# The first nine steps of a retention and mixture-of-depths kernel: one chunk of 128 tokens a step in place of two of 64

## The chip, the cores and the metric

The kernel runs on one core of a Trainium2 chip. Its time is the device time of one execution in microseconds (us). The kernel before was timed three times: 277.89, 277.18 and 274.35 us, median 277.18. One further execution was profiled: 274.87 us, of which 273.2 us are the span that the profile covers. Shorter is better.

## The reference

Eight batches, eight heads, 576 tokens, 64 numbers a head; everything is float32. First a retention layer with decay gamma by head, then a mixture-of-depths layer on the 512 numbers of a token:

```python
scores = scale * np.matmul(q, k.transpose(0, 1, 3, 2))
Dmat = np.where(rel >= 0, gamma[:, None, None] ** rel[None, :, :], 0.0)
x = np.matmul(scores * Dmat[None], v)          # then heads side by side: (8, 576, 512)
s = np.einsum('bsd,d->bs', x, w_gate)
out = x.copy()
for b in range(B):
    top_idx = np.argpartition(-s[b], 128)[:128]
    xe = x[b, top_idx]
    ye = np.maximum(xe @ w1, 0.0) @ w2         # 512 -> 1024 -> 512
    g = 1.0 / (1.0 + np.exp(-s[b, top_idx]))
    out[b, top_idx] = xe + g[:, None] * ye
```

So every token gets its retention value, and the 128 tokens of each batch with the highest gate scores get an MLP on top.

## The kernel before

**Retention by chunks.** A chunk is 64 tokens of one batch, all heads; a batch has 9 chunks. A step `s` takes two chunks, so 36 steps do all 72, and a batch ends after 4.5 steps. The host packs q and k (transposed), v and k for a step into one 1 MB block, `raw[s]`: [128, 4, 512], heads 0 to 3 on one half of the partitions and heads 4 to 7 on the other. In a step:

- `scaled` (L151, on POOL; in steps 5 to 7 on ACT in eight pieces, L147): v times a power of gamma, `vs`.
- `scores` (L175): 16 matmuls of 64x64, k against q, into PSUM `sc_ps`.
- `masked` (L232, DVE): causal mask, PSUM to SBUF `am`.
- `update` (L165): 16 matmuls add k times v to the running state `u_ps`; `copied` (L205, ACT) brings the state to SBUF, `st`, after each chunk.
- `crosswise` (L186, L196): 32 matmuls into `y_ps`: the masked scores times `vs`, and q times the state before the chunk. They are recorded one step late, between the scores and updates of the next step (`block`), so that PE need not wait for the mask.
- `values` (L241, L250, DVE): `y_ps` times a power of gamma to `xs`, and the gate score of each token as sums over two half rows.
- `store` (L259, POOL queue): `xs` to the output, two transfers a step.

**Choice of tokens for a batch.** `total` (L281) adds the half sums, `spread` (L296, L301) puts the 576 scores in a row on every partition, five `compare` (L309, DVE) count for each token how many score higher, `one_hot` (L322, DVE) and `rows` (L330) turn the ranks into 128 row numbers, and `gather` (L339, an indirect transfer on the POOL queue) reads these rows of the output back. It must wait until the batch's stores have landed. For batch 0 two special steps, `first` (s = 4) and `second` (s = 5), do part of this early.

**MLP for a batch.** `turn` (L356) transposes the gathered rows, four `up` parts (L365, 16 matmuls of 128x128 each) and four `down` parts (L373, 4 matmuls with 512 columns each) follow, and a scatter writes the rows. The parts are dealt out over the steps of the following batches, one or two at the end of a step (`share`); batch 0's start in step 8, batch 1's in step 13, batch 2's in step 18.

**Order.** Each engine runs its instructions in the order in which the Python code issues them; nothing is rescheduled. Loads go through the SP queue, stores and gathers through the POOL queue. `raw` has 8 buffers: step s+7's load waits for step s-1. `bring` issues loads in pieces of 256 KB; for steps 0 to 5 (`few`) it lets a piece wait for an earlier one, so that at most five are under way:

```python
while len(flying) > 3 + few:
    flying.popleft()
if few and len(flying) == 4:
    tc.add_manual_dep(ins, flying.popleft().name, ...)
```

Of the kernel before, what the change touches and what calls it, by code (L numbers as in the profile page):

```python
# [16 lines left out]
P = 128  # L17
TINY = 2.0**-125
C = 64
# [4 lines left out]
def layout(H, NC, cap):  # L24

    at, n = {}, 0
    for name, size in (("dec", 2 * (NC + 1) * H // 2), ("causal", C), ("wgh", H * C // 2),
                       ("pair", C), ("place", (NC + 1) // 2)):
        at[name] = n
        n += size  # L30
    at["end"] = n
    return at
# [3 lines left out]
def kernel(  # L36
# [16 lines left out]

    nc = tc.nc
# [13 lines left out]
    assert cap == P and cap < S <= 1024 and NC % 2 == 1  # L68
# [20 lines left out]
    flying = deque()  # L89

    def bring(out, in_, few=False):

        ins = nc.sync.dma_start(out=out, in_=in_).ins
        while len(flying) > 3 + few:
            flying.popleft()
        if few and len(flying) == 4:
            tc.add_manual_dep(
                ins, flying.popleft().name,
                mybir.DependencyInfo(mybir.DependencyClass.Sync, mybir.DependencyReason.DATA),
                reason="few transfers at a time")  # L100
        flying.append(ins)

    def load(s):
        x = loads.tile([P, 4, DM], F32, name="raw")
        for a in range(4):
            bring(x[:, a, :], qkvk[s, :, a * DM : (a + 1) * DM], few=s <= ends[0])
        raw[s] = x
# [5 lines left out]
    place = const.tile([P, NK], F16, name="place")  # L113

    dec = table[:, : col["causal"]].rearrange("p (s h) -> p s h", s=2)
# [4 lines left out]
    ahead = const.tile([P, 2 * S - C], F32, name="ahead")  # L120
    slots = const.tile([P, cap], F32, name="slots")
    eye = const.tile([P, P], F32, name="eye")
    ones = const.tile([P, P], F32, name="ones")

    def constants():

        nc.gpsimd.memset(ahead, -TINY)
        nc.gpsimd.affine_select(out=ahead, in_=ahead, pattern=[[-1, 2 * S - C]],
                                compare_op=OP.is_gt, fill=0.0, base=S - C, channel_multiplier=1)
        nc.gpsimd.memset(ones, 1.0)  # L130
        nc.gpsimd.affine_select(out=eye, in_=ones, pattern=[[-1, P]],
                                compare_op=OP.is_equal, fill=0.0, base=0, channel_multiplier=1)
        nc.gpsimd.iota(slots, pattern=[[1, cap]], base=0, channel_multiplier=0,
                       allow_small_or_imprecise_dtypes=True)
# [5 lines left out]
    by_act = lambda s: ends[0] <= s < ends[0] + 3  # L140

    def scaled(s):
        c = batch(2 * s)[1]
        vs[s] = work.tile([P, DM], F32, name="vs")
        if by_act(s):
            for i in range(H):
                nc.scalar.activation(  # L147
                    out=vs[s][:, D * i : D * i + D], in_=raw[s][:, 2, D * i : D * i + D],
                    func=AF.Copy, scale=dec[:, 0, HH * c + i : HH * c + i + 1])
            return  # L150
        nc.gpsimd.tensor_tensor(  # L151
            out=blocks(vs[s]), in0=blocks(raw[s][:, 2, :]),
            in1=dec[:, 0, HH * c : HH * c + H].unsqueeze(2).to_broadcast([P, H, D]), op=OP.mult,
        )
# [115 lines left out]
    full = S // P  # L270
    size = lambda k: P if k < full else S - P * full
# [16 lines left out]
    def spread(b, *groups):  # L288

        if b not in row:  # L290
            row[b] = work.tile([P, S], F32, name="row", bufs=2)
        for group in groups:
            t = bank("row_ps")
            at = 0
            for k, p0, p1 in group:
                nc.tensor.matmul(  # L296
                    t[:, at : at + p1 - p0], rs[b][p0:p1, k : k + 1].to_broadcast([p1 - p0, P]),
                    eye[p0:p1, p0:p1], start=True, stop=True, skip_group_check=True)
                at += p1 - p0
            j = P * group[0][0] + group[0][1]  # L300
            nc.scalar.copy(out=row[b][:, j : j + at], in_=t[:, :at])  # L301

    def compare(b, k, j0=0, j1=S, part=0):
        if b not in rank:
            rank[b] = work.tile([P, 2, NK], F32, name="rank", bufs=2)
        n = size(k)
        scr = work.tile([P, S], F32, name="scr2", bufs=1)
        at = S - C - P * k
        nc.vector.scalar_tensor_tensor(  # L309
            scr[:n, : j1 - j0], row[b][:n, j0:j1], rs[b][:n, k : k + 1],  # L310
            ahead[:n, at + j0 : at + j1],
            op0=OP.subtract, op1=OP.is_gt, accum_out=rank[b][:n, part, k : k + 1])
# [5 lines left out]
    def one_hot(b):  # L318
        hot[b] = work.tile([P, NK, cap], F16, name="hot", bufs=2)
        for n, ks in ((P, slice(0, full)), (size(full), slice(full, NK))):  # L320
            m = ks.stop - ks.start
            nc.vector.tensor_tensor(  # L322
                out=hot[b][:n, ks, :], in0=slots[:n].unsqueeze(1).to_broadcast([n, m, cap]),
                in1=rank[b][:n, 0, ks].unsqueeze(2).to_broadcast([n, m, cap]), op=OP.is_equal)

    def rows(b):
        t = bank("idx_ps")
        for k in range(NK):
            n = size(k)
            nc.tensor.matmul(t[:, :1], hot[b][:n, k, :], place[:n, k : k + 1],  # L330
                             start=k == 0, stop=k == NK - 1)
        idx[b] = work.tile([P, 1], I32, name="idx", bufs=B)
        nc.scalar.copy(out=idx[b], in_=t[:, :1])
# [71 lines left out]
    columns = lambda k0, k1: [(k, 0, size(k)) for k in range(k0, k1)]  # L405
# [3 lines left out]
    def go(fs):  # L409
        for f in fs:  # L410
            f()

    def first():

        s = ends[0] - 1
        block(s)
        masked(s)
        go(crosswise(s, (0,)))
        values(s - 1)
        store(s - 1)  # L420
        total(0, 0, NC - 1)
        spread(0, columns(0, full))
        values(s, (0,))
        total(0, NC - 1, NC)
        spread(0, columns(full, NK))
        go(crosswise(s, (1,)))
        for k in range(full):
            compare(0, k, 0, P * full)

    def second():  # L430
        s = ends[0]
        block(s, False)
        masked(s)
        for k in range(full):
            compare(0, k, P * full, S, 1)
        compare(0, full)
        joined(0, full)
        one_hot(0)
        values(s - 1, (1,))
        store(s - 1)  # L440

    s = ends[0] + 1
    plan(mid, s, rows, 0)
    plan(mid, s, gather, 0)
    plan(early, s + 1, turn, 0)
    plan(late, s + 1, mlp, 0)
    plan(late, s + 1, gates, 0)
    start = [s + 2]
    for b in range(1, last):
        s = ends[b]  # L450
        plan(late, s, total, b)
        plan(early, s + 1, spread, b, columns(0, full), columns(full, NK))
        for k in range(3):
            plan(late, s + 1, compare, b, k)
        for k in range(3, NK):
            plan(mid, s + 2, compare, b, k)
        plan(mid, s + 2, one_hot, b)
        plan(late, s + 2, rows, b)
        plan(late, s + 2, gather, b)
        plan(early, s + 4, turn, b)  # L460
        plan(early, s + 4, mlp, b)
        plan(late, s + 4, gates, b)
        start.append(s + 4)
    plan(late, NS - 1, total, last, 0, NC - 2)
    plan(before, NS, spread, last, columns(0, odd) + [(odd, 0, C)])
# [15 lines left out]
    bring(table, consts)  # L481
    constants()
    for s in range(AHEAD):
        load(s)
    for d in range(KD):
        bring(w1_sb[:, d, :], w1[P * d : P * d + P])
    bring(wg, bass.AP(tensor=w_gate.tensor, offset=w_gate.offset, ap=[[0, P], [1, DM]]))
    scaled(0)
    for s in range(NS + 1):
        if s and s + AHEAD - 1 < NS:  # L490
            load(s + AHEAD - 1)
        if s == 2:
            for d in range(0, FB, 2):
                bring(w2_sb[:, d : d + 2, :],
                      w2[P * d : P * d + 2 * P].rearrange("(a p) d -> p a d", p=P))
        run(before, s)
        if s + 1 < NS and not by_act(s + 1):
            scaled(s + 1)
        if s == ends[0] - 1:
            first()  # L500
        elif s == ends[0]:
            second()
        else:
            block(s)
            if s < NS:
                masked(s)
            run(mid, s)
            if s:
                values(s - 1)
                store(s - 1)  # L510
        if s == 2:
            nc.vector.tensor_copy(out=place, in_=place_f)
        if by_act(s + 1):
            scaled(s + 1)
# [6 lines left out]
    spread(last, [(odd, C, P)], [(full, 0, C)])  # L521
# [3 lines left out]
    compare(last, full)  # L525
# [70 lines left out]
```

## Time and profile before

| | us |
|---|---|
| three timed runs | 277.89, 277.18, 274.35 |
| profiled execution | 274.87 |
| its span | 273.2 |
| busy in the span: PE / DVE / POOL / ACT | 231.0 / 141.7 / 103.3 / 58.7 |
| first scores (L175) | 5.88 |
| masks of steps 0 to 4 | 7.9, 11.7, 15.7, 21.2, 27.4 |
| masks of steps 5 to 9 | 37.8, 42.3, 47.2, 59.3, 64.8 |
| raw loads of 256 KB, median from issue to landing | 5.2 |
| bytes moved | 56.8 MB |

A group line of the profile has the line in the code, the engine, the operation, what it writes and reads, the shapes, the count; then the busy time in us and the mean ns of one; then the idle time of the engine ahead of it and what ended most of it. In the chain of waits each line has a start in us, a length, and what ran or was waited for; "issue" is time in which an engine waited for nothing that the profile shows. The granted clock is the share of full speed that TensorE was given.

### The profile page before, as it was taken

How to read it: one execution, taken by the hardware profiler on the slowest of the kernel's cores; microseconds unless marked ns; L12 is line 12 of the kernel's file. 1: busy time of each engine (PE TensorE's matmuls, PEld its weight loads, DVE VectorE, ACT ScalarE, POOL GpSimd, SP SyncE). 2: the span in 40 equal slices, each digit the busy share in tenths (PEclk: the TensorE clock that was granted, in tenths of full speed). 3: DMA queues.
4: the chain of work that ended last, by engine and by line, in shares of the span. 5: the costliest groups of instructions: out<-in, count | busy, mean ns of one | idle time of the engine just before them, and what ended most of it. 6: DMA issues, size and time to landing. Idle time of an engine off the chain costs nothing.

```text
span 273.2 us, 11548 instructions
## 1 busy us (share of the span) xinstructions
PE 231.0 (85%) x5184; PEld 183.9 (67%) x5184; DVE 141.7 (52%) x354; ACT 58.7 (22%) x182; POOL 103.3 (38%) x138
## 2 busy tenths in 40 slices
PE   1845886089977999969999999699999998999992
PEld 1734785079753897649866986469868975894950
DVE  0333585243593538865864378818736487750101
ACT  1111164032210232113211231112212321121100
POOL 4264202804407353364163741824165525201101
PEclk9998568569998999999999999979999999999998
DMA  6879999999996786586577766866042113211000
GB/s 209 276 244 304 315 409 377 376 406 385 326 390 198 245 280 213 190 277 247 170 229 250 256 218 207 266 221 216 26 114 80 42 43 78 70 49 38 38 2 38
DMA packets 27601, 56.83 MB, mean 208 GB/s; under 512 B 4000, under 2 KB 4128, under 8 KB 27552
## 3 DMA queue, kind: packets, MB, share of 16 engines
q1 hardware_dynamic: 22688, 42.46, 46.6%
q0 software_dynamic: 4864, 13.64, 15.2%
q8 instruction: 41, 0.67, 1.0%
q14 instruction: 8, 0.07, 0.1%
HBM read 44.54 MB, written 11.53 MB: 205 GB/s over the span
## 4 chain that ended last, share of the span: by engine, by line
PE 60%; issue 14%; DMA 13%; DVE 8%; ACT 1%; POOLq 1%; POOL 1%; SPq 0%; DVEq 0%; ACTq 0%
PE h_ps L365 17%; PE ye_ps L373 11%; PE u_ps L165 9%; PE sc_ps L175 9%; DMA xr<-out,idx 7%; DVE scr L309 5%; DMA raw<-in_qkvk 5%; PE row_ps L296 5%; PE y_ps L196 4%; PE y_ps L186 3%; PE xg_ps L356 2%; DVE hot L322 1%; DVE am L232 1%; DMA out<-xs 1%; PE idx_ps L330 1%
## 5 line engine op out<-in xcount | busy, mean ns | idle before, releaser
L259 POOL DMA_DIRECT2D out<-xs x64 | 39.8, 625 | 90.3 <-DVE xs L241 89.9
L232 DVE TENSOR_TENSOR am<-sc_ps,table 128x512 f32<-128x512 f32 x36 | 24.9, 690 | 74.2 <-PE sc_ps L175 53.6
L365 PEld LDWEIGHTS h_ps<-xg,w_sb 128*128 128x128 f32 x512 | 59.5, 192 | 5.5 <-issue 4.4
L373 PE MATMUL ye_ps<-w_sb,hT 128*128 128x512 f32 x128 | 63.0, 624 | 0.0
L365 PE MATMUL h_ps<-xg,w_sb 128*128 128x128 f32 x512 | 62.2, 278 | 0.5 <-issue 0.4
L175 PE MATMUL sc_ps<-raw 64*64 64x64 f32 x1152 | 44.9, 231 | 11.0 <-DMA raw<-in_qkvk 5.9
L175 PEld LDWEIGHTS sc_ps<-raw 64*64 64x64 f32 x1152 | 41.0, 146 | 13.1 <-issue 7.0
L165 PE MATMUL u_ps<-vs,raw 64*64 64x64 f32 x1024 | 45.7, 232 | 3.3 <-ACT st L205 2.4
L186 PE MATMUL y_ps<-vs,am 64*64 64x64 f32 x1152 | 45.9, 232 | 3.0 <-issue 2.7
L309 DVE SCALAR_TENSOR_TENSOR scr<-row,rs,ahead 128x576 f32<-128x576 f32 (+5 forms) x47 | 42.7, 909 | 10.2 <-ACT row L301 6.1
L165 PEld LDWEIGHTS u_ps<-vs,raw 64*64 64x64 f32 x1024 | 38.1, 144 | 11.7 <-issue 6.4
L186 PEld LDWEIGHTS y_ps<-vs,am 64*64 64x64 f32 x1152 | 40.1, 144 | 3.6 <-issue 3.0
L205 ACT COPY st<-u_ps 128x256 f32<-128x256 f32 x64 | 23.7, 371 | 82.3 <-PE u_ps L165 60.9
L196 PE MATMUL y_ps<-st,raw 64*64 64x64 f32 x1024 | 39.7, 227 | 2.0 <-issue 2.0
L151 POOL TENSOR_TENSOR vs<-raw,table 128x512 f32<-128x512 f32 x33 | 34.7, 1052 | 13.3 <-DMA raw<-in_qkvk 12.8
L196 PEld LDWEIGHTS y_ps<-st,raw 64*64 64x64 f32 x1024 | 36.0, 143 | 2.1 <-issue 2.1
L373 PEld LDWEIGHTS ye_ps<-w_sb,hT 128*128 128x128 f32 x128 | 22.8, 195 | 19.5 <-issue 18.7
L250 DVE SCALAR_TENSOR_TENSOR scr<-xs,table 128x256 f32<-128x256 f32 x72 | 34.0, 473 | 2.5
L241 DVE TENSOR_TENSOR xs<-y_ps,table 128x512 f32<-128x512 f32 (+1 forms) x37 | 24.7, 667 | 3.9 <-PE y_ps L196 3.6
L367 ACT ACTIVATE hT<-h_ps 128x256 f32<-128x256 f32 x32 | 12.3, 383 | 55.7 <-PE h_ps L365 55.7
L378 DVE SCALAR_TENSOR_TENSOR o<-ye_ps,gate,xr 128x512 f32<-128x512 f32 x8 | 6.0, 751 | 30.3 <-PE ye_ps L373 17.5
L379 POOL DMA_INDIRECT out<-o,idx x8 | 9.5, 1187 | 31.1 <-DVE o L378 31.1
(35 smaller groups left out, 113.0 us busy)
## 6 DMA issues: line engine op xcount, KB each, us to landing
raw<-in_qkvk SPq DMA_DIRECT2D x144, 256.0 KB, 5.2
out<-xs POOLq DMA_DIRECT2D x64, 128.0 KB, 4.9
w_sb<-in_w SPq DMA_DIRECT2D x8, 512.0 KB, 8.9
out<-xs POOLq DMA_DIRECT2D x16, 64.0 KB, 4.9
wg<-in_w_gate SPq DMA_DIRECT2D x1, 256.0 KB
table<-in_consts SPq DMA_DIRECT2D x1, 234.5 KB
xr<-out,idx POOLq DMA_INDIRECT x8, 4.0
out<-o,idx POOLq DMA_INDIRECT x8, 4.1
```

The lines of the kernel that those rows point to most:

```text
L151: nc.gpsimd.tensor_tensor(out=blocks(vs[s]), in0=blocks(raw[s][:, 2, :]), in1=dec[:, 0, HH * c : HH * c + H].unsqueeze(2).to_broadcast([P, ...
L165: yield lambda h=h, half=half: nc.tensor.matmul(u_ps[b][half, where(0, h)], raw[s][half, 3, where(e, h)], vs[s][half, where(e, h)], start= ...
L175: yield lambda e=e, h=h, half=half: nc.tensor.matmul(sc_ps[s][half, where(e, h)], raw[s][half, 1, where(e, h)], raw[s][half, 0, where(e, h ...
L186: yield lambda e=e, h=h, i=i, half=half: nc.tensor.matmul(y_ps[s][halves[1 - i], where(e, h)], am[s][half, where(e, h)], vs[s][half, where ...
L196: yield lambda g=g, e=e, h=h, i=i, half=half: nc.tensor.matmul(y_ps[s][halves[1 - i], where(e, h)], raw[s][half, 0, where(e, h)], st[g - 1 ...
L232: nc.vector.tensor_tensor(out=blocks(am[s]), in0=blocks(sc_ps[s]), in1=causal.unsqueeze(1).to_broadcast([P, H, C]), op=OP.mult)
L241: nc.vector.tensor_tensor(out=blocks(xs[s])[:, i0:i1, :], in0=blocks(y_ps[s])[:, i0:i1, :], in1=dec[:, 1, HH * c + i0 : HH * c + i1].unsqu ...
L250: nc.vector.scalar_tensor_tensor(scr, xs[s][:, W * e : W * e + W], 1.0, wgh, op0=OP.mult, op1=OP.mult, accum_out=sc[b][:, c : c + 1])
L259: nc.gpsimd.dma_start(out=outs[b][C * c : C * c + 2 * C, W * i : W * i + W] .rearrange("(c p) d -> p c d", c=2), in_=x)
L309: nc.vector.scalar_tensor_tensor(scr[:n, : j1 - j0], row[b][:n, j0:j1], rs[b][:n, k : k + 1], ahead[:n, at + j0 : at + j1], op0=OP.subtrac ...
L365: nc.tensor.matmul(t[:, a, :], w1_sb[:, d, P * (f + a) : P * (f + a) + P], xg[b][:, d, :], start=d == 0, stop=d == KD - 1)
L373: nc.tensor.matmul(ye[b], hT[b][:, a, :], w2_sb[:, a, :], start=a == 0, stop=a == FB - 1)
```

## The change

The first nine steps, which are the first two batches (2 x 576 = 9 x 128 tokens), get their own code. A step takes 128 tokens in their order as one chunk, with tokens on partitions. Step 4 (`middle`) holds the last 64 tokens of batch 0 and the first 64 of batch 1, kept apart by its own mask. There are 32 matmuls a step and one state copy. The scaling of v runs on POOL in all steps. Row sums come out of `values` directly, without `total`. Everything of a step, its `within` matmuls too, is issued in that step, so `block(9)` has no crosswise of step 8. Batch 0's whole ranking is in step 5, its rows and gather in step 6, its transposes at the end of step 7 and its MLP from step 8 on, as before; batch 1's follow one step earlier than before (MLP from step 12). Loads are 512 KB each, with no limit; w1 and w2 come in loads of 1 MB, issued behind the loads of steps 8 and 9 (before: w1 ahead of step 8's load, w2 behind step 9's). The table is 144 columns longer and comes in two parts. A sigmoid on one column runs first on ACT.

```diff
-    def bring(out, in_, few=False):
...
     def load(s):
         x = loads.tile([P, 4, DM], F32, name="raw")
-        for a in range(4):
-            bring(x[:, a, :], qkvk[s, :, a * DM : (a + 1) * DM], few=s <= ends[0])
+        for a in (0, 2):
+            nc.sync.dma_start(out=x[:, a : a + 2, :], in_=qkvk[s, :, a * DM : (a + 2) * DM])
...
+    middle = NC // 2
+    heads = [(hh, j) for j in range(HH) for hh in range(2)]
+    def big_scores(s):
+        am[s] = work.tile([P, H, P], F32, name="am2", bufs=2)
+        sc_ps[s] = [bank("sc_ps", "sc", 2) for _ in range(2)]
+        for hh, j in heads:
+            half = halves[1 - hh]
+            nc.tensor.matmul(
+                sc_ps[s][hh][:, P * j : P * j + P], raw[s][half, 1, P * j : P * j + P],
+                raw[s][half, 0, P * j : P * j + P], start=True, stop=True, skip_group_check=True)
+    def big_masked(s):
+        for hh in range(2):
+            nc.vector.tensor_tensor(
+                out=am[s][:, HH * hh : HH * hh + HH, :],
+                in0=sc_ps[s][hh].rearrange("p (h d) -> p h d", d=P),
+                in1=seen[:, int(s == middle), :].unsqueeze(1).to_broadcast([P, HH, P]),
+                op=OP.mult)
+    def big_update(s):
...
+        for hh, j in heads:
+            h = HH * hh + j
+            nc.tensor.matmul(
+                u_ps[b][halves[1 - hh], where(0, j)], raw[s][rows_, 3, D * h : D * h + D],
+                vs[s][rows_, D * h : D * h + D], start=new and j == 0,
+                stop=s in (middle - 1, NC - 2), skip_group_check=True)
+        st[2 * s + 1] = work.tile([P, W], F32, name="st")
+        nc.scalar.copy(out=st[2 * s + 1], in_=u_ps[b][:, :W])
+    def big_before(s):
...
+        for hh, j in heads:
+            half = halves[1 - hh]
+            nc.tensor.matmul(
+                y_ps[s][hh][:n, where(0, j)], raw[s][half, 0, P * j : P * j + n],
+                st[2 * s - 1][half, where(0, j)], start=s != middle and j == 0,
+                stop=s == middle, skip_group_check=True)
+    def big_within(s):
+        for hh in range(2):
+            for j in range(HH):
+                h = HH * hh + j
+                nc.tensor.matmul(
+                    y_ps[s][hh][:, where(0, j)], am[s][:, h, :], vs[s][:, D * h : D * h + D],
+                    start=s in (0, middle) and j == 0, stop=s != middle, skip_group_check=True)
+    def big_values(s):
+        xs[s] = work.tile([P, DM], F32, name="xs", bufs=4)
+        for hh in range(2):
+            i = HH * hh
+            nc.vector.tensor_tensor(
+                out=blocks(xs[s])[:, i : i + HH, :], in0=blocks(y_ps[s][hh])[:, :HH, :],
+                in1=big[:, 1, s, i : i + HH].unsqueeze(2).to_broadcast([P, HH, D]), op=OP.mult)
+        scr = work.tile([P, DM], F32, name="scr3", bufs=1)
+        nc.vector.scalar_tensor_tensor(scr, xs[s], 1.0, wg, op0=OP.mult, op1=OP.mult,
+                                       accum_out=rs01[:, s : s + 1])
...
-    def first():
...
-    def second():
...
+    def big_step(s):
+        big_ahead(s)
+        if s == middle + 1:
+            spread(0, columns(0, 0, NK - 1), columns(0, NK - 1, NK))
+        if s == middle + 2:
+            rows(0)
+            gather(0)
+        big_masked(s)
+        big_rest(s)
+        if s == middle + 1:
+            for k in range(NK):
+                compare(0, k)
+            one_hot(0)
+        big_values(s)
+        big_store(s)
...
+    warm = work.tile([P, 1], F32, name="warm", bufs=1)
+    nc.scalar.activation(out=warm, in_=ones[:, :1], func=AF.Sigmoid)
     for s in range(AHEAD):
         load(s)
+        if s == 0:
+            nc.sync.dma_start(out=wg, in_=bass.AP(...))
+        if s == 2:
+            nc.sync.dma_start(out=table[:, n_big:], in_=consts[:, n_big:])
...
+        if s < NC:
+            big_step(s)
         else:
-            block(s)
+            block(s, s > NC)
```

`big_ahead(s)` issues the scores, `big_before` (q times the state) and `big_update`, in this order; `big_rest(s)` issues `big_within`. In step 4, `big_before` comes after `big_within`. `big_store` writes 128 rows in one transfer (two in step 4). The two banks of `sc_ps` and the two of `y_ps` are all that these steps have, so step s+1's scores wait for step s's masks, and its `before` for step s's values.

## The prediction

> **What bounds the kernel now.** I read first the page's strip of 40 slices (6.83 us each), to see where TensorE is not full.
>
> ```profile
> PE   1845886089977999969999999699999998999992
> PEclk9998568569998999999999999979999999999998
> GB/s 209 276 244 304 315 409 377 376 406 385 326 390 198 245 280 213 190 277 247 170 229 250 256 218 207 266 221 216 26 114 80 42 43 78 70 49 38 38 2 38
> ```
>
> From the tenth slice on PE is nearly always full. Before it PE has holes, and the granted clock falls to 0.5 and 0.6. The transfers move 209 to 315 GB/s in the first five slices and about 380 after that: the start runs below what the queues can carry. The table of stretches says the same.
>
> ```profile
> 20.00:30.00 10.00, 6.24 (x212) 5.91 (x212) 4.38 (x12) 0.74 (x2) 3.84 (x7) 0.74 0.93 306
> 30.00:40.00 10.00, 8.60 (x163) 7.82 (x164) 6.01 (x23) 4.69 (x20) 1.09 (x2) 0.58 1.01 371
> 63.70:118.90 55.20, 51.21 (x1367) 40.08 (x1366) 35.52 (x82) 11.81 (x36) 24.18 (x32) 0.97 0.81 269
> ```
>
> (length, busy PE, PE weight load, DVE, ACT, POOL, clock, transfer share, GB/s). Steps 9 to 17 fill 63.7 to 118.9 us, and there PE is busy for 51.2 of 55.2 us at clock 0.97. The change rewrites the steps before that. The chain of waits, in order of time, says what they wait for.
>
> ```profile
> 2.19 4.26 DMA raw<-in_qkvk
> 6.46 3.46 DMA raw<-in_qkvk
> 9.94 5.18 DMA raw<-in_qkvk
> ...
> 18.64 1.79 issue
> ...
> 23.27 2.89 issue
> ...
> 44.18 1.99 issue
> ...
> 48.73 6.85 DMA xr<-out,idx
> ```
>
> Loads first, then "issue" holes, then batch 0's gather, for which PE stands still 7.5 us (48.15 to 55.63). The issue holes have a count behind them: numbering PE's instructions in order of time, they stand before the 451st, 707th, 963rd and 1,730th, multiples of 256 apart (within one), and the instruction queue moved 41 packets of 16 KB, one for each 256. So PE ran out of fetched instructions: a stretch of small matmuls uses 256 faster than they come.
>
> The line from which both kernels run nearly the same code is the start of step 9, at 63.7 us, behind two parts of batch 0's MLP:
>
> ```profile
> 59.94 3.77 PE h_ps L365 x32
> 63.70 0.20 PE sc_ps L175 x2
> ```
>
> **The change, part by part.** I work out when step 9 starts in the changed kernel.
>
> *First data.* The third transfer in the trace (0.76 MB with those ahead of it) landed at 5.74 us and later ones 0.64 to 0.70 us per 256 KB: bytes flow from about 3.8 us on at 0.38 to 0.4 MB/us. Now a 74 KB table piece and 512 KB of q and k come first: 0.6 MB, 5.3 us; v and k follow at 6.7 us. Transfers of one queue land in order (the four w_sb loads, issued at 31.1 to 33.0 us, land 1.1 to 1.3 us apart behind the raw loads ahead of them), so "no limit" doesn't delay the first.
>
> *Step 0.* Scores 5.4 to 6.7, masks to 7.9, v scaled on POOL (1.05) by 7.8, within to 9.7 (PE at half clock, as in the first step of before), values to 11.0, masks of step 1 to 12.4 us.
>
> *The loop of steps 1 to 8.* PE now waits in each step for its own masks; before, the crosswise matmuls came one step late. DVE in one step:
>
> ```profile
> L232 DVE TENSOR_TENSOR am<-sc_ps,table 128x512 f32<-128x512 f32 x36 | 24.9, 690 | 74.2 <-PE sc_ps L175 53.6 <-PE y_ps L196 17.4 <-PE y_ps L186 3.2
> L347 DVE SCALAR_TENSOR_TENSOR scr<-xr,wg 128x512 f32<-128x512 f32 x8 | 5.5, 682 | 5.8 <-DMA xr<-out,idx 5.8
> L241 DVE TENSOR_TENSOR xs<-y_ps,table 128x256 f32<-128x256 f32 x2 | 0.8, 417 | 0.2 <-PE y_ps L196 0.2
> ```
>
> Two masks at 0.69, two values at 0.417, one score sum at 0.68 + 0.08: 2.97 us, plus 0.1 for the semaphore after the second mask: 3.1 us a step if PE hides. Before it was 0.69 + 0.68 + 2 x 0.55 = 2.5. PE has 32 matmuls. The trace has no 64-row tile with 128 columns in pairs; bounds: a pair runs together (112 ns, as one 128-column h_ps matmul) or one after the other (224). Two 64x64 start 7 ns apart and a pair takes 57 ns, so I take pairs together: scores 0.45 (or 0.9), before and update 0.24 each (or 0.47), within 8 x 0.06 = 0.47; 1.4 us (or 2.3). The old 64 took 64 x 28 ns = 1.8 us. PE thus gains little by itself; at half clock it needs 2.8 (or 4.6) and shows in the loop. PE sits idle about half of each step, and the trace fell to half clock at 24.7 and 45.2 us after stretches of 3.4 us that were 45 and 56% busy, and came back only after stretches of 86 to 100%. A loop that idles at full clock and fills at half will swing: I take 3.5 us, between 3.1 and 5.0.
>
> The Trainium skill (TensorE: Matmul & The Clock Gate, section "HAM oscillation — how this bites in real kernels") warns that idle gaps over about 3.4 us drop the clock; by that rule alone no gap here is long enough and the loop would stay at 3.1.
>
> *Tile modes.* 64x128, 128x64 and 128x128 now alternate three times a step. From a 128x128 h_ps to a 64x64 update the next matmul starts 205 ns later, not 112: 0.09 us a switch, 0.27 a step, inside the wait for the masks; bare it is 2.4 us over nine steps.
>
> *Step 5* carries batch 0's ranking whole: 4 compares at 0.83, one of 64 rows at 0.83, one-hot 0.9: 5.0 us on DVE, with PE waiting for values(5). *Gather:* idx stands 2.3 us after step 5's one-hot (31.4: values, before, update, rows, copy), about 33.7 us; the gather takes 6.85 us as before, 40.6; PE gets there at 38.9, so it stalls 1.7 us in place of 7.5. The stores it waits for are issued by 25 us, not at 43.
>
> *Sum:* 12.4 + 6 x 3.5 + 5.0 + 0.5 = 38.9, stall to 40.6, transposes 0.6, scores, masks and within of step 8 2.8: 44.0; two MLP parts 3.77: 47.8; something for half clock there and in steps 0 to 4: **step 9 starts at 49** (63.7 before). Issue holes: 64 instructions a step make 256 last 13 us; none. The sigmoid load (1.28 us at 57.4, which held a state copy from 57.84 to 58.79) goes: 0.9 us, already inside the 49. The Trainium skill (ScalarE: Activation LUTs, "What ACT_TABLE_LOAD costs") counts a drain of 1.38 us with each load, 2.66 in all; by it the gain would be 1.7 us more, but here the copy began 0.13 us after the load ended. The eight small scalings on ACT in each of steps 5 to 7 go to POOL (1.05 us each), which has one store a step at 0.6 beside them: hidden.
>
> *Transfers set the ceiling.* Until raw 10 the queue carries 0.07 + 11 x 1.05 + 0.5 (wg, rest of the table) + 4.2 (w1, w2) = 16.3 MB, and about 2.5 MB of stores and gather go beside it: 18.8 MB at 0.38 MB/us from 3.8 us on is 53.3 us. Step 10 starts by PE at 49 + 6.0 - 0.9 = 54.1 (69.7 before). So loads follow by a hair, and more than 16.4 us can't be won. From step 11 on a step needs 1.3 MB, 3.5 us, and PE takes 5 to 6.
>
> *From step 9 on* work and order are the same, but for crosswise(8), already done (32 x 28 ns = 0.9 us), batch 1's row sums, and its MLP a step earlier; by step 18 both have done the same parts. So 63.7 - 49 + 0.9 = **15.6 us** stay.
>
> The profiled execution took 274.87 us (span 273.2); 274.87 - 15.6 = 259.3. It lies 2.3 below the median of 277.18; I add half: **260.5**.
>
> **The rivals.**
> - *Half clock, pairs one after the other:* PE needs 4.6 us, the loop 5.0. Step 9 at 49 + 7 x 1.5 = 59.5; gain 5.1; 270. For it: clock 0.58 at 30 to 40 us with PE 86% busy. Against: the 7 ns starts. 0.18.
> - *Loads at 300 GB/s*, as in slices 4 and 5: raw 10 at 3.8 + 18.8 / 0.3 = 66.5, gain 3.2, about 272. Against: 376 to 409 as soon as the limit was gone. 0.10. The edit not doing what it says (transfers sharing instead of in order: first scores at 12.7 with 3.4 MB in flight) costs under 7.4 us and lies between.
> - *Slower: the loop becomes one serial chain at half clock.* Scores 1.8, before and update 1.9, masks 1.4, within 0.95, values 1.6, semaphores 0.4: about 8 us a step with nothing beside it; step 9 at 49 + 7 x 4.5 = 80.5, plus 3.8 for cold MLP parts; 295. It decides from 49 + 7 x (c - 3.5) = 64.6, c = 5.7 us a step, and is slower by 2% from c = 6.5. For it: PE waits for DVE in each step. Against: score banks are free after the masks, so scores run under values. 0.07.
>
> **The numbers.** The forecast has 0.65. About 2% can be told from no change: 271.6 and 282.7 us. Low end: loop 3.1 and loads at the ceiling, 274.87 - 17.3, and PE's wait of 1.38 us at 79 us for batch 1's one-hot saved: 256, less 2 for spread: 254. High end: the first rival, 270. Faster 0.65 + 0.16 + 0.03 = 0.84; same 0.09; slower 0.07.
>
> **What would show it.** First scores near 5.4 us; masks 3.1 to 4 us apart in steps 1 to 4; 9 us between the masks of steps 5 and 6; no issue hole before 49 us; a PE stall under 3 us ahead of batch 0's transposes; 380 GB/s from the second slice on; step 9 near 49 and step 18 near 103 us (118.9). It is wrong if masks lie over 5.7 us apart, or if PE from step 9 on waits for raw.

## The result and the profile after

| | before | after |
|---|---|---|
| median of the runs, us | 276.06 (274.35 to 277.89) | 299.50 (297.29 to 300.50) |
| profiled execution / its span, us | 274.87 / 273.2 | 299.89 / 298.2 |
| start of step 9's scores, us | 63.7 | 83.3 |
| start of step 18's mask, us | 118.4 | 138.4 |
| start of step 27's mask, us | 174.7 | 198.4 |
| PE busy in the span, us | 231.0 | 269.8 |

The kernel became slower: ratio 1.084, interval 1.073 to 1.094. Medians in this text are of all executions, while a ratio to the kernel before, which ran beside each experiment, leaves out executions over 1.5% above the fastest of their kernel. Of the 25 us between the two profiled executions, 19.7 us stand at step 9 already, and 0.3 us are added up to step 18. Another 3.7 us come between steps 18 and 27, where the code is the same in both kernels, and 1.3 us later.

First the page's strip of 40 slices of the kernel after (7.46 us each).

```profile
PE   1999999699999998796999998969999999999993
PEclk9999999955899999899799999997999999999997
GB/s 201 394 403 418 410 397 406 164 206 182 164 52 143 192 301 262 147 213 291 199 181 191 235 267 182 185 269 210 206 40 75 77 70 2 111 70 27 45 0 35
```

The holes in PE are gone, and the transfers run at about 400 GB/s from the second slice on, as forecast. From the eighth slice on they fall to 164 GB/s: loads are no longer asked for, because the steps come too slowly. PE is full, and the time is lost in PE itself. The table of stretches (length, busy PE, PE weight load, DVE, ACT, POOL, clock, transfer share, GB/s) says how few matmuls fill it.

```profile
20.00:30.00 10.00, 10.00 (x73) 9.53 (x74) 3.29 (x8) 0.37 (x1) 1.66 (x2) 1.00 1.03 417
60.00:70.00 10.00, 10.00 (x87) 9.50 (x87) 3.91 (x8) 0.43 (x2) 3.79 (x5) 0.50 0.55 186
83.25:138.90 55.65, 51.65 (x1299) 39.88 (x1298) 33.31 (x79) 11.77 (x35) 21.93 (x29) 0.97 0.61 188
```

PE is TensorE, DVE VectorE, ACT ScalarE and POOL GpSimd. 73 matmul records, which are the matmul entries of the trace, keep PE busy for 10 us. Steps 9 to 17 (the last line) take 55.7 us, against 55.2 before, so the second half of the work is not what changed. The chain of waits, in order of time (start, length, what ran), shows what one costs.

```profile
21.46 2.01 PE sc_ps L157 x16
23.47 1.60 PE y_ps L193 x16
25.07 1.05 PE u_ps L179 x16
26.12 3.61 PE y_ps L202 x16
...
62.27 3.61 PE y_ps L202 x16
...
77.73 1.97 PE y_ps L202 x16
79.70 3.63 PE h_ps L457 x32
83.33 0.72 PE sc_ps L259 x19
```

Lines 157, 193, 179 and 202 are scores, `before`, update and `within`. Step 2, the first four lines, is these four pieces end to end, 8.27 us, with no wait for DVE between them. The same 16 records of `within` take 3.61 us at 26 us and at 62 us, and 1.97 us at 77.7 us. At 62 us the table above gives the clock as 0.50, and at 77.7 us it is full. So the clock was at half at 26 us too, although the strip has a 9 there and the table a 1.00: the first change of clock that the trace holds is at 52.7 us, and ahead of the first change the strip and the table show full speed whatever the clock is. By the distances between matmul records (213 ns in `within` at 26 us) the clock was at half from the start to 52.7 us, and again from 59.5 to 76.6 us.

DVE, which the forecast took for the bound of the loop, has these groups (count, then busy us, mean ns, and the idle time ahead of them).

```profile
L163 DVE TENSOR_TENSOR am<-sc_ps,seen 128x512 f32<-128x512 f32 x18 | 11.6, 684 | 13.6 <-PE sc_ps L157 13.6
L223 DVE TENSOR_TENSOR xs<-y_ps,table 128x256 f32<-128x256 f32 x18 | 7.4, 422 | 31.3 <-PE y_ps L202 27.1 <-PE y_ps L193 4.2
L227 DVE SCALAR_TENSOR_TENSOR scr<-xs,wg 128x512 f32<-128x512 f32 x9 | 6.2, 691 | 0.3
```

The durations are the forecast's (0.69, 0.417 and 0.68 us). But DVE waits 45 us for PE in these nine steps, not PE for DVE. The masks of steps 0 to 4 start at 8.2, 15.2, 23.5, 31.8 and 40.4 us, 7.0 to 8.6 us apart: over the 5.7 us that the forecast named as a sign of being wrong. The one PE wait over 0.4 us of the loop is at step 5's ranking: 2.9 us, 56.0 to 59.0.

### The profile page after: what moved, and what is told of

It is laid out like the page before. It is cut to its first block, busy times and chain, and to the rows that moved or that the text cites. A ratio compares the mean times of both kernels' runs of the same rounds, so it can differ in the third digit from the quotient of the medians.

```text
span 298.2 us, 10283 instructions
## 1 busy us (share of the span) xinstructions
PE 269.8 (90%) x4630; PEld 220.3 (74%) x4630; DVE 147.4 (49%) x345; ACT 48.7 (16%) x145; POOL 101.3 (34%) x134
## 4 chain that ended last, share of the span: by engine, by line
PE 71%; issue 12%; DMA 7%; DVE 6%; POOLq 1%; POOL 1%; ACT 1%; SPq 0%; DVEq 0%
PE h_ps L457 15%; PE ye_ps L465 12%; PE y_ps L202 9%; PE u_ps L249 7%; PE sc_ps L259 6%; DMA xr<-out,idx 4%; PE row_ps L386 4%; PE sc_ps L157 4%; PE y_ps L193 4%; DVE scr L399 3%; PE y_ps L280 3%; PE u_ps L179 2%; DMA raw<-in_qkvk 2%; PE y_ps L270 2%; PE xg_ps L448 1%
## 5 line engine op out<-in xcount | busy, mean ns | idle before, releaser
L399 DVE SCALAR_TENSOR_TENSOR scr<-row,rs,ahead 128x576 f32<-128x576 f32 (+3 forms) x43 | 39.5, 919 | 13.5 <-ACT row L391 12.2
L249 PE MATMUL u_ps<-vs,raw 64*64 64x64 f32 x768 | 33.0, 222 | 0.1
L249 PEld LDWEIGHTS u_ps<-vs,raw 64*64 64x64 f32 x768 | 26.9, 135 | 8.4 <-issue 7.3
L270 PE MATMUL y_ps<-vs,am 64*64 64x64 f32 x864 | 31.5, 221 | 0.0
L259 PE MATMUL sc_ps<-raw 64*64 64x64 f32 x864 | 30.2, 219 | 0.0
L202 PE MATMUL y_ps<-vs,am 128*128 128x64 f32 x144 | 29.7, 392 | 0.1
L202 PEld LDWEIGHTS y_ps<-vs,am 128*128 128x128 f32 x144 | 28.1, 300 | 1.1 <-DVE am L163 0.3
L259 PEld LDWEIGHTS sc_ps<-raw 64*64 64x64 f32 x864 | 27.7, 135 | 1.6 <-issue 1.5
L270 PEld LDWEIGHTS y_ps<-vs,am 64*64 64x64 f32 x864 | 27.6, 135 | 0.1
L157 PE MATMUL sc_ps<-raw 64*128 64x128 f32 x144 | 17.7, 418 | 6.0 <-DMA raw<-in_qkvk 6.0
```

Source lines behind the costliest of these rows:

```text
L157: nc.tensor.matmul(sc_ps[s][hh][:, P * j : P * j + P], raw[s][half, 1, P * j : P * j + P], raw[s][half, 0, P * j : P * j + P], start=True, ...
L202: nc.tensor.matmul(y_ps[s][hh][:, where(0, j)], am[s][:, h, :], vs[s][:, D * h : D * h + D], start=s in (0, middle) and j == 0, stop=s != ...
L249: yield lambda h=h, half=half: nc.tensor.matmul(u_ps[b][half, where(0, h)], raw[s][half, 3, where(e, h)], vs[s][half, where(e, h)], start= ...
L259: yield lambda e=e, h=h, half=half: nc.tensor.matmul(sc_ps[s][half, where(e, h)], raw[s][half, 1, where(e, h)], raw[s][half, 0, where(e, h ...
L270: yield lambda e=e, h=h, i=i, half=half: nc.tensor.matmul(y_ps[s][halves[1 - i], where(e, h)], am[s][half, where(e, h)], vs[s][half, where ...
L399: nc.vector.scalar_tensor_tensor(scr[n, : j1 - j0], row[b][n, j0:j1], rs[b][n, k : k + 1], ahead[n, at + j0 : at + j1], op0=OP.subtract, o ...
```

## The experiments

Two theories stood at the start: the price of PE's matmuls and its clock, or the new loads, which changed as well. In a timeline of PE, `128*128 128x64` means 128 rows and 128 weight columns of the array, then 128 rows and 64 moving columns: the weights stand in the array, and the moving columns stream through it.

### A warm clock ahead of the loop, with the new and with the old code

```diff
+    t = bank("warm_ps")
+    for _ in range(12):
+        nc.tensor.matmul(t[:, :P], ones, ones, start=True, stop=True, skip_group_check=True)
     for s in range(AHEAD):
```

> The changed kernel with 12 matmuls of 128x128 on a constant tile ahead of step 0, while PE waits for the first load; nothing else is different. Theory: PE is the bound in steps 1 to 8 (8.2 us a step, no idle time) and runs them at half clock; at full clock a step takes about 4.3 us. Then step 9 starts near 52 us, not 83, and the time is about 268 us; if the clock falls again inside the loop, something between 268 and 299. Rival (fixed latencies, waits for DVE or loads make the 8.2 us): no change, 297 to 301.

> The kernel before with the same 12 matmuls ahead of step 0. Theory: its first 11 us run at half clock and end 2 us earlier, and loads then hold the steps: 272 to 277 us. It is the control for the first run: a gain there of over 10 us more than here belongs to the new steps.

With the new code: 285.2 us (278.4 to 287.7; they spread too far for an interval), some 14 us under the kernel after, whose lowest is 297.3. With the old code: 275.2 us, ratio 0.989 (0.976 to 1.002), no sure gain. Two stretches of the first one:

```profile
16.00:24.00 8.00, 8.00 (x124) 7.66 (x120) 5.05 (x12) 0.75 (x2) 3.28 (x4) 1.00 1.03 414
48.00:60.00 12.00, 12.00 (x84) 11.63 (x84) 3.26 (x7) 0.71 (x3) 2.72 (x3) 0.50 1.03 410
```

In the first, 124 records fit in 8 us, where the kernel after has 64. Here the changes of clock are in the trace: full from 5.4 us, half from 29.3 us, full again from 63.4 us. Step 3 takes 4.48 us at full clock, and the masks of steps 6 and 7, at half, start 8.4 us apart. So the loop does not pull the clock up, but it keeps it up, until PE waits in step 4:

```profile
27.86 2.44 PE L202 MATMUL y_ps<-vs,am 128*128 128x64 f32 x16 [1.47 <-DVE am L163]
```

The wait, in brackets, is for step 4's masks. On DVE they stand behind two small `place` instructions that the code issues at the end of step 3 and that end at 27.2 us. The clock falls at 29.3 us, ahead of step 5's ranking. After that it does not come back for 34 us, with PE busy for 12.00 of 12.00 us in the stretch shown. A low clock explains much of the loss. It doesn't explain why a full PE leaves the clock low.

### More columns, and so more work, in the same matmuls

In `before` and `within` three of four matmuls get 128 moving columns in place of 64 (the expectations say seven of eight; the code has three of four). The further columns land where nobody reads, and `values` reads every second block of 64; its 422 ns stay the same.

```diff
+            w = P if j < HH - 1 else D
             nc.tensor.matmul(
-                y_ps[s][hh][:n, where(0, j)], raw[s][half, 0, P * j : P * j + n],
-                st[2 * s - 1][half, where(0, j)], start=s != middle and j == 0,
+                y_ps[s][hh][:n, P * j : P * j + w], raw[s][half, 0, P * j : P * j + n],
+                st[2 * s - 1][half, D * j : D * j + w], start=s != middle and j == 0,
...
-                    y_ps[s][hh][:, where(0, j)], am[s][:, h, :], vs[s][:, D * h : D * h + D],
+                    y_ps[s][hh][:, P * j : P * j + w], am[s][:, h, :], vs[s][:, D * h : D * h + w],
```

> The changed kernel with 128 moving columns in place of 64 in seven of eight 'before' and 'within' matmuls (the second 64 land in columns of the bank that nobody reads; the output is the same). Theory: a pass costs 2 cycles times the larger of its weight columns and its moving columns, and here 128 weight columns set it, so at the same clock a step stays at 8.2 us; and the clock stays low because these passes stream only half of the time, so with more columns it may rise: 268 to 299 us, not slower. Rival (moving columns set the price): 2.4 us a step more, 318 us.

Measured 280.3 us, ratio 1.012 (1.001 to 1.023): up to twice the streaming, and 19 us less than the kernel after. The timeline of PE in step 3 (start, length, line, shapes, count):

```profile
22.04 1.16 PE L157 MATMUL sc_ps<-raw 64*128 64x128 f32 x16
23.04 1.01 PE L194 MATMUL y_ps<-st,raw 64*128 64x128 f32 x16
23.97 0.69 PE L179 MATMUL u_ps<-vs,raw 128*64 128x64 f32 x16
24.59 2.00 PE L204 MATMUL y_ps<-vs,am 128*128 128x128 f32 x16
26.52 0.38 PE L157 MATMUL sc_ps<-raw 64*128 64x128 f32 x2
```

The same 16 records of `within` with 64 moving columns, in step 3 of the warm kernel:

```profile
22.69 2.00 PE L202 MATMUL y_ps<-vs,am 128*128 128x64 f32 x16
```

Two things follow. With 128 weight columns, 64 moving columns cost as much as 128: consecutive `within` records mostly start 112 ns apart in both at full clock and 213 ns in both at half. So not the moving columns set the price here; that the weights do is tested by the split below. And a busy PE is not enough for the clock: PE is as busy as in the kernel after, more columns stream, and the clock is full from 13.2 us on.

The same edit in `before` alone:

> The changed kernel with 128 moving columns in seven of eight 'before' matmuls alone ('within' stays at 64; output the same). Theory: at half clock the clock rises after a window of 3.4 us in which columns stream for more than about 76% of the time; the changed kernel's windows in the loop reach 51 to 74%. The wider 'before' adds 0.74 us of streaming to a step of 8.2 us at no price, so windows of up to 80% come, and the clock rises within two steps: 278 to 286 us. Rival (the rise in e2_wide came from 'within', or from something else than the streaming share): 295 or more.

Measured 280.3 us, ratio 1.024 (1.016 to 1.032). It is the expected size, but the first rise in the profiled execution is not the edit's doing: the clock is full from 9.9 us on, and the first wider matmul, in step 1's `before`, starts later:

```profile
12.73 1.01 PE L193 MATMUL y_ps<-st,raw 64*128 64x128 f32 x16
```

Up to there PE's matmuls are those of the kernel after. By the count below, the window ahead of the rise has a share of 0.72, the lowest that rose, so this rise was luck. What the edit shows in this profile is the return. The clock falls at 30.4 us, behind a wait of 1.47 us in step 4, and at 44.0 us, behind one of 3.02 us for the ranking, and is back after 3.4 and 10.2 us. In the warm kernel, without the wider matmuls, it took 34.1 us. All four executions lie at 277.6 to 282.9 us and those of the kernel after at 297.3 or more, so the gain does not rest on that luck alone.

The changes of clock lie multiples of 3.41 us apart (52.7, 59.5 and 76.6 us in the kernel after). To put a number on the rule I cut the first 90 us of all fourteen kernels into windows of that length and worked out for each the share of time in which moving columns stream. I counted 0.83 ns a column and record at full clock and twice that at half; the records with 512 moving columns, 430 ns apart at full clock, give 0.84. At half clock 87 windows had shares up to 0.80 and were followed by half; 35 had 0.72 or more and were followed by full. At full clock 25 windows had 0.44 or less and were followed by half; 208 had 0.38 or more and stayed. So in these traces the clock rises from about three quarters and falls below about four tenths; between 0.72 and 0.80 it did either. The loop of the kernel after streams 0.51 to 0.74 of a window in steps 1 to 4: enough to keep a full clock, not enough to get one.

### The weights of `within` in two halves

Each `within` matmul with 128 weight columns becomes two with 64, side by side in the array; the step has 40 matmuls.

```diff
-                nc.tensor.matmul(
-                    y_ps[s][hh][:, where(0, j)], am[s][:, h, :], vs[s][:, D * h : D * h + D],
+                for half in halves:
+                    nc.tensor.matmul(
+                        y_ps[s][hh][half, where(0, j)], am[s][:, h, half],
+                        vs[s][:, D * h : D * h + D],
...
```

> The changed kernel with each 'within' matmul (128 weight columns, 64 moving) cut into two with 64 weight columns each, on the two column halves of the array; the output is the same and there are 40 matmuls a step, not 32. Theory (the larger of weight and moving columns sets the price, halves run together): 'within' takes 1.7 us a step at half clock, not 3.4, and 1.0 at full clock, not 1.9; with streaming share up from 62 to 78% the clock may rise. 286 us if it stays at half, about 270 if it rises. Rival (a price by matmul or by moving columns): 299 or more.

Measured 267.4 us (266.8 to 267.9), ratio 0.977 (0.970 to 0.984). One edit turns the loss into a gain. The timeline of PE in step 2:

```profile
14.85 1.16 PE L157 MATMUL sc_ps<-raw 64*128 64x128 f32 x16
15.85 1.01 PE L193 MATMUL y_ps<-st,raw 64*128 64x64 f32 x16
16.78 0.69 PE L179 MATMUL u_ps<-vs,raw 128*64 128x64 f32 x16
17.30 1.30 PE L203 MATMUL y_ps<-vs,am 128*64 128x64 f32 x32
18.52 0.72 PE L157 MATMUL sc_ps<-raw 64*128 64x128 f32 x8
```

`within` takes 1.22 us (17.30 to 18.52) in place of 1.93 at full clock, a step 3.67: with the same moving columns, half the weight columns a record make it cheaper, so the loading of the weights did set the price. The window from 7.6 to 11.0 us, in which step 0's `within` begins, streams 0.82, and those of steps 1 to 4 stream 0.66 to 0.79. The clock is full from 11.0 us on, but for 38.3 to 41.7 us behind the ranking, and step 9 starts at 54.2 us.

### The loads

The old code with the new loads (512 KB, no limit, sigmoid table first), and the old code with its 256 KB loads and only the limit gone:

```diff
-        for a in range(4):
-            bring(x[:, a, :], qkvk[s, :, a * DM : (a + 1) * DM], few=s <= ends[0])
+        for a in (0, 2):
+            bring(x[:, a : a + 2, :], qkvk[s, :, a * DM : (a + 2) * DM])
...
+    warm = work.tile([P, 1], F32, name="warm", bufs=1)
+    nc.scalar.activation(out=warm, in_=ones[:, :1], func=AF.Sigmoid)
```

That is the edit of the first; the second keeps the old line, with `few=False`.

> The kernel before with the change's loads alone: 512 KB pieces, no limit, sigmoid first; steps of two 64-token chunks as they were. Theory: the loads are no part of the loss; 268 to 278 us. Rival (loads without limit crowd out stores, gathers and instruction fetches): 285 us or more.

> The kernel before with its 256 KB loads and no limit. It tells apart what made e3_before_loads slower: if the missing limit did (v and k behind more bytes, instruction fetches behind more bytes), 280 to 285 us again; if the 512 KB pieces did (q and k usable only when 512 KB are there), 273 to 277.

283.2 us, ratio 1.019 (1.007 to 1.032), and 277.5 us, ratio 1.014 (1.004 to 1.023). Both are slower than before; the first missed the expected times and lies between the theories. The chain of waits of the first one (start, length, what):

```profile
1.72 7.29 DMA raw<-in_qkvk
9.05 0.10 issue
9.15 1.05 POOL vs L151
10.25 1.14 PE u_ps L165 x16
```

v and k of step 0 land at 9.0 us, and step 1's mask starts at 14.7 us in place of 11.7. The largest issue hole is longer too, 3.50 us against 2.89. With only the limit gone the mask of step 1 starts at 13.3 us, the clock goes full at 14.7 us in place of 11.1, and step 9's mask comes 3.0 us later. So the new loads cost the old code some 2%. Most of that seems to be the limit, but the two intervals overlap.

The new code with the old loads and limit:

```diff
-        for a in (0, 2):
-            nc.sync.dma_start(out=x[:, a : a + 2, :], in_=qkvk[s, :, a * DM : (a + 2) * DM])
+        for a in range(4):
+            bring(x[:, a, :], qkvk[s, :, a * DM : (a + 1) * DM], few=s <= ends[0])
...
```

> The changed kernel with the loads of before: 256 KB pieces and the limit up to step 5. Theory: PE has no idle time in steps 1 to 4, so loads hold nothing up there and the time stays: 296 to 302 us. Rival (the loads carry a good part of the loss, as e3_before_loads would have it with its 8 us): 290 to 293.

The executions took 277.0, 290.8, 294.3 and 295.4 us: three lie 4 to 9 us under the median of the kernel after and one 22, so neither range holds. The one of 295.4 us is profiled. There the clock has the same pattern as after (half to 51.9 us), step 9's mask comes at 83.8 against 84.5 us, and the rest of the difference arises after step 9. So the new loads don't explain the first 20 us; whether they cost a few stays open. No profile shows the execution of 277.0 us. An early rise of the clock like the one at 9.9 us above would fit it, but that is not shown.

### Put together

The split with the warm clock, and batch 0's ranking dealt over steps 5 and 6 behind the values, its gather in step 7 and its transposes in step 8; then the same with the wide `before`; the split with the wide `before` alone; and last the limit and 256 KB loads on top.

```diff
-        if s == middle + 2:
+        if s == middle + 3:
             rows(0)
             gather(0)
         big_masked(s)
         big_rest(s)
+        big_values(s)
+        big_store(s)
         if s == middle + 1:
-            for k in range(NK):
+            for k in range(3):
                 compare(0, k)
+        if s == middle + 2:
+            for k in range(3, NK):
+                compare(0, k)
             one_hot(0)
-        big_values(s)
-        big_store(s)
...
-    plan(late, s, turn, 0)
-    plan(late, s, mlp, 0)
+    plan(early, s + 1, turn, 0)
+    plan(early, s + 1, mlp, 0)
```

> The changed kernel with the 12 matmuls ahead, 'within' split as in e5_split, and batch 0's ranking dealt out: values of step 5 ahead of the compares, two compares and the one-hot in step 6, gather in step 7, transposes in step 8. Theory: about 3.7 us a step at full clock, step 9 near 48 us, 262 us (258 to 268). If the clock falls in the loop as in e1_warm_after: 270 to 278.

> e7_best with the wider 'before'. In e7_best's profile the clock fell at 36.3 us and came back only at 56.8; with a larger share of streaming it should be back after one or two windows: 257 to 262 us. Rival: 264 to 267 as e7_best.

> e5_split with the wider 'before'. Theory: same prices, so at most the stretch of half clock after the wait in step 5 gets shorter: 264 to 268 us. Rival (wider matmuls cost time at full clock): 270 or more.

> e9_best_wide with the loads of before (256 KB, limited up to step 5). PE is no longer at half clock, so loads can matter now: if the limit helps, as it does in the kernel before, 2 to 4 us less than e9_best_wide; if the steps of 3.7 us now wait for loads that the limit slows, 3 us more or worse.

| split, and with it | us, median and spread | ratio to before | step 9's mask | from there to the end |
|---|---|---|---|---|
| nothing | 267.4 (266.8 to 267.9) | 0.977 (0.970 to 0.984) | 55.4 | 210.7 |
| warm, ranking dealt | 265.8 (259.2 to 266.8) | unclear | 60.0 | 205.0 |
| warm, dealt, wide | 267.2 (265.5 to 271.0) | 0.971 (0.965 to 0.977) | 57.9 | 210.2 |
| wide | 270.1 (267.9 to 271.3) | 0.982 (0.974 to 0.990) | 54.8 | 214.0 |
| warm, dealt, wide, limit | 269.2 (268.8 to 269.7) | 0.981 (0.977 to 0.985) | 61.8 | 205.3 |

The last three came out above what was expected of them. The wide columns are free, as priced (16 records take 1.01 us with 64 and with 128), and step 9's mask comes earlier with them, by 0.6 us without and by 2.1 us with the warm clock and the dealt ranking. Their effect on the clock is mixed: without those two the half clock behind the ranking lasts 6.8 us in place of 3.4, since a window with a share of 0.77 did not rise. Dealing out the ranking only moves PE's wait for it: 2.9 us in step 6 in place of 3.9 in step 5. Behind it the version without the wide columns is at half clock from 36.3 to 56.8 us, and the one with them from 38.4 to 41.8 and, behind a wait of 1.8 us for the gather, from 52.1 to 55.5 us; both start step 9 later than the plain split. The limit brings nothing here. What differs more is the time from step 9's mask to the end: 205 to 215 us over all kernels, with nearly the same code there. It holds waits, mostly of 2 to 4 us, for gathers in steps 18 and 27 and in most kernels windows at half clock behind them. Why they fall as they do stays open. Versions within 5 us of each other are not ranked by these runs. What the intervals do show is that four of the five beat the kernel before, by 1.8 to 2.9%, and with it the kernel after.

## Why the prediction was wrong

**The step that failed** is PE's price: "The old 64 took 64 x 28 ns = 1.8 us", and the new 32 "1.4 us (or 2.3)". The group of the masked half of the old crosswise matmuls, in the kernel before, shows the first half of the fault (count, busy us, mean ns, idle):

```profile
L186 PE MATMUL y_ps<-vs,am 64*64 64x64 f32 x1152 | 45.9, 232 | 3.0 <-issue 2.7 <-DVE am L232 0.2
```

36 steps with 16 such matmuls are 576. Each stands twice, and so does every float32 matmul of both kernels, the transposes aside (the 16 and 4 matmuls of an MLP part in the text on the kernel before are records as well). The 28 ns are those of a record. The old step took 128 x 28 = 3.6 us, not 1.8. The same count stands in "64 instructions a step make 256 last 13 us": a step has 64 matmul records and 64 weight loads, so 256 last two steps.

The second half is the weights. I priced `within` at 8 x 0.06, by its 64 moving columns, and `before` at 0.24, as pairs of that length. Both have 128 weight columns, which cost as much as 128 moving ones. At full clock (step 3 of the warm kernel) the four pieces take 1.00, 0.93, 0.62 and 1.93 us, 4.48 in all. The forecast had 0.45, 0.24, 0.24 and 0.47. So even at full clock PE, and not DVE with its 3.1 us, is the bound of the loop. The change replaces 3.65 us of PE a step (64 pairs 57 ns apart) by 4.48, 23% more, and about as much at half: 8.27 for 128 x 53 ns = 6.8 (the old code's pairs start 107 ns apart there). The 7 ns between the starts of a pair were read rightly: of the first rival the half clock came, the pairs one after the other did not.

The Trainium skill (TensorE: Matmul & The Clock Gate, section "LDWEIGHTS (loading the stationary operand)") has the rule that I passed over: a weight load lasts as long as its columns, about P / 1.2 ns for P of them. By it 128 columns take 107 ns, an estimate; the runs show 105 ns from pair to pair and 112 from full tile to full tile at full clock, and 207 and 213 at half, where the rule is too low.

**The clock** was the larger part. "A loop that idles at full clock and fills at half will swing: I take 3.5 us" failed in that the loop, once full, did not swing back. PE waits for weights for a quarter to a half of its time, so the streaming share stays at 0.51 to 0.74. Seven ordinary steps at 8.27 in place of 3.5 us are 33.4 us: 6.9 by the price at full clock (4.48 in place of 3.5) and 26.5 by the half clock. Step 9 came 34.3 us after the forecast's 49. The warm kernel, the two wide ones and the split show it, since each changes only the clock or the shape of the matmuls, with the same loads and steps, and takes 14 to 32 us away. The rule that the forecast quoted, of the same page's section "HAM oscillation — how this bites in real kernels", warns of idle gaps. Here the clock stayed low from 8.5 to 52.7 us, and PE had no gap of 0.3 us in that time: measured, the absence of gaps is not enough.

**What held.** First scores at 6.0 us (5.4 forecast); no issue holes before 49 us; about 400 GB/s from the second slice; DVE's durations; no PE stall at batch 0's gather (1.7 forecast). But 11.9 us lie between the masks of steps 5 and 6, not 9, and the 0.9 us that were to be won behind step 9 didn't come: steps 9 to 17 take 55.65 us against 55.20. The transfers' ceiling of 16.4 us was never reached. The sigmoid table and the MLP a step earlier were not tried alone.

**The rivals.** The third, "one serial chain at half clock", was right in the clock, the size ("about 8 us a step", 8.27), the place (80.5 plus 3.8, measured 83.3) and the end (295, measured 299.5). That the place fits is in part luck: the 3.8 us for cold MLP parts didn't come (3.63 us, no more than in the kernel before), and 2.8 us came in step 0 instead, with step 1's mask at 15.2 and not 12.4 us. Its mechanism was wrong: it gave `within` 0.95 us and added 3.4 us of DVE work and semaphores. PE alone fills the step, `within` with 3.61 us, and DVE lies beside it. Its chance of 0.07 rested on DVE. The condition, c = 5.7 us a step, was the right one to look at, and with weight columns priced like moving ones the trace of before could have given c: by the 112 ns of an h_ps record the four pieces are 0.9 + 0.9 + 0.45 + 1.8 us at full clock and twice that, 8.1, at half. The second, loads at 300 GB/s, didn't happen.

## What to carry to other kernels

Before pricing matmuls, divide a group's count by the calls in the code, and price each record by the larger of its weight and its moving columns: fewer matmuls are no gain if each loads twice the weights. A loop in which TensorE mostly loads weights can be completely busy and still stay at half clock; here splitting the weights, or streaming columns that nobody reads, brought the clock up. Trust the granted clock only behind its first change in the trace, and check it by the time of one known matmul.

## What the runs showed of the hardware

- The clock goes by streaming, not by being busy, with a gap between rising (from 0.72 to 0.80 of a window of 3.41 us) and falling (below 0.38 to 0.44). Up to twice as many streamed columns in half of a step's matmuls made the kernel 19 us faster.
- Two tiles with 64 weight columns each, side by side, mostly take 59 ns for the pair at full clock (7 and 52 ns between starts); one tile with 128 takes 112, for the same result.
- The limit on loads under way is worth 1.4% (0.4 to 2.3) to the old code. Without it the transfers move more bytes in the first 30 us, 343 against 263 GB/s, and the first steps still come later.
